# A new order for the first part of a Performer and Fourier-mixing kernel, from a planner with other costs and a lock list for the shared port

## The chip, the cores and the metric

The kernel runs on one core of one Trainium2 chip. The metric is the time of one execution on the device in microseconds (us). Before the change it is 1139.51 us, the median of three runs (1139.21 to 1140.97).

The engines of a core run side by side, each through its own list of instructions in order: TensorE (PE, matmuls; PEld is its weight load), VectorE (DVE), ScalarE (ACT) and GpSimd (POOL). SyncE (SP) is used as a queue that issues DMA transfers. An instruction that waits holds up all that stand behind it on its engine.

## What is computed

An attention block with positive random features, and a Fourier mixing block with a two-layer network behind it, all in float32, on 8 sequences of 576 tokens, 8 heads of 64 and a model width of 512:

```python
def phi(x):                                  # m = 128 features
    proj = np.einsum('bhsd,md->bhsm', x, omega)
    h = proj - np.sum(x * x, axis=-1, keepdims=True) / 2.0
    return np.exp(h - np.max(h, axis=-1, keepdims=True)) / np.sqrt(m)
q_p, k_p = phi(q * scale), phi(k * scale)
kv = np.einsum('bhsm,bhsd->bhmd', k_p, v)
z = np.sum(k_p, axis=2)
x = einsum('bhsm,bhmd->bhsd', q_p, kv) / (einsum('bhsm,bhm->bhs', q_p, z)[..., None] + 1e-06)
# heads side by side: x is (8, 576, 512)
u = x + np.real(np.fft.fft(np.fft.fft(x, axis=1), axis=2))
un = (u - mean(u)) / np.sqrt(var(u) + 1e-06)
out = u + np.maximum(un @ w_ch1, 0.0) @ w_ch2        # 512 -> 2048 -> 512
```

The weights w_ch1 and w_ch2 come as 64-bit floats and are narrowed to 32 bits on the chip.

## The kernel before

The work has two parts. The **first part** holds the attention of all 32 pairs of heads, the Fourier mixing of the 8 sequences, the narrowing of the weights, the network for the first 4 tiles of 128 tokens in the plain way, and the preparation of what the second part needs. The **second part** does the network for the other tokens in 8 blocks of 512, with a two-level scheme of sums and seven products in place of eight (lines L1454, L1596 and L1839 are its matmuls).

In the first part these streams run side by side:

- `attn` (three streams, pair n in stream n mod 3): q and k of a pair come in one tile `kq` and are transposed on TensorE (L524, groups of 4, 4 and 1 matrices), the transposed blocks are copied out of PSUM by ScalarE or VectorE (`evicted`, L538 and L540), projected on the features (`pairs_of`, L618), the row maxima are taken on VectorE (`softmax`, L561) and the exponentials on ScalarE (L578); the key-value products follow (L652) with a copy (`keep`, L666 and L668), the transposes of the query features (L524 again, out with `order`), the numerators and denominators (L699 and L707), and the division on VectorE or ScalarE (L716 to L728).
- `mix` (one stream over the 8 sequences): `folds` adds and subtracts rows on VectorE or GpSimd (L755 to L791), two rounds of matmuls with cosine and sine tables (L811 and L821, then L861 and L872), and `residual` adds the result to x (`summed`, L922 and L923) and stores u in DRAM.
- `weights` and `narrow`: 32 pieces of the weights are loaded as pairs of 32-bit words and put together by ScalarE or GpSimd, VectorE (L454 to L461), and a last add on GpSimd or VectorE (L467).
- `plain`: the network for the first 4 tiles, L1127 with w1 and L1150 with w2, with `hidden` between them (L1111 and L1113).
- `w2_parts`: differences of blocks of w2 for the second part (L1292, on VectorE or GpSimd), in seven sets; each set ends with five stores into `w2l` in DRAM from SyncE's queue (L1315 and L1317), and the next set rewrites the buffers that those stores read.
- `loads`, `loads_v`, `load_tables`: the loads of k, q, v (L388, L391, L396) and of the tables. `kq` has two buffers, v three.

TensorE uses different tile shapes for these steps, which the planner calls modes: "whole" (128x128: transposes, mixing, plain network), "rows" (64x128: projections of the first six pairs), "quarters" (64x64: the other projections and the key-value products) and "halves" (128x64: numerators, and the last part of a mixing).

The order of all instructions is set by hand-made planning. Each stream is a Python generator that yields a `Step` (engine or engines with a cost each, the events it waits for, buffers that it takes and gives, DMA size) and then writes its instructions. `Listing.run` keeps the list `todo` of the steps that stand next in each stream, chooses one, moves a clock for its engine, and lets the generator write the instructions, so that each engine's program is in the order of choice. In the first part the choice is not made by the clock but read from a string, `PICKS`: letter by letter, the index in `todo` is the letter's place modulo 36, and a letter of place 36 or more (a capital) sets `other`. Where a step may run on two engines, `other` chooses between them. In the second part there are no picks, and the step that can begin first is taken, within a slack, by its due time.

The clock still has a say in the first part where a step has two engines: before the change these are ranked by the time at which each would finish, and `other` takes the second of that rank. The clock's rows are in `FIRST`: the fourth figure, `turn`, is added to a TensorE step whose mode differs from that of the step before. Steps marked `port=True` read and write SBUF on VectorE or GpSimd; by `free[PORT]` none of them begins, in the planner's clock, before the one listed last has ended.

## Time and profile before

| what | value |
|---|---|
| median of three runs | 1139.51 us |
| the profiled execution's own time | 1138.29 us |
| its span | 1136.3 us |
| granted TensorE clock | 0.999 |
| first part on TensorE (start to the last L1150) | 0 to 421.5 us |
| busy in the first 423 us: PE, DVE, ACT, POOL | 410.6, 342.1, 281.1, 175.2 us |
| busy from 423 to 1136.3 us: PE, DVE, ACT, POOL | 705.5, 529.8, 263.4, 248.4 us |
| DMA, mean over the span | 227 GB/s |

The times of the profile count from the start of the span. A row of the chain of work that ended last gives a start, the time until the next piece of the chain, and the instructions in it. A row of waits gives the waiting engine, tile and line, what ended the wait, then the total, the number and the longest. A row of the order of time gives start and length. "Busy" for TensorE is modelled from the start of one matmul to the next and includes what a matmul is held up inside the engine.

### The profile page before, as it was taken

What the parts mean: (1) busy time and instruction counts of PE and PEld (TensorE: products, weight loads), DVE (VectorE), ACT (ScalarE), POOL (GpSimd) and SP (SyncE); (2) the same over time, 40 slices, a digit from 0 to 9 for tenths busy, and PEclk for the clock granted to TensorE, in tenths of its full rate; (3) what the DMA queues carried; (4) which work ended last, traced back from release to release, by engine and by line L of the source; (5) the groups of instructions that cost most, each with busy time, mean ns of one, the idle gap of its engine ahead of it and who ended that gap; (6) DMA issues with size and microseconds to landing.
All of it is one profiled execution on the core that took longest, in us unless ns stands there. A gap on an engine that the chain in (4) does not pass through costs nothing.

```text
span 1136.3 us, 34262 instructions
## 1 busy us (share of the span) xinstructions
PE 1116.1 (98%) x13639; PEld 1039.7 (91%) x13640; DVE 871.9 (77%) x1735; ACT 544.6 (48%) x1646; POOL 423.5 (37%) x435
## 2 busy tenths in 40 slices
PE   8999999999999999989999999999999999999998
PEld 7778888879868768989999999999999999999998
DVE  6999899987576646787777678678678678678666
ACT  7898898856535216724424424423523522522311
POOL 2443443553573124512711710720630540550361
PEclk9999999999999999999999999999999999999999
DMA  7856766575663238597797797798698798788576
GB/s 241 229 184 178 225 181 199 176 216 173 206 203 120 84 109 266 184 320 248 220 333 242 212 333 250 205 314 275 199 302 276 222 288 291 216 264 296 185 224 203
DMA packets 187965, 258.28 MB, mean 227 GB/s; under 512 B 52384, under 2 KB 83360, under 8 KB 187808
## 3 DMA queue, kind: packets, MB, share of 16 engines
q1 hardware_dynamic: 187312, 255.85, 72.2%
q8 instruction: 108, 1.77, 0.6%
q14 instruction: 49, 0.40, 0.1%
q10 hardware_dynamic: 496, 0.26, 0.1%
HBM read 212.27 MB, written 47.97 MB: 229 GB/s over the span
## 4 chain that ended last, share of the span: by engine, by line
PE 92%; DVE 2%; DMA 2%; ACT 2%; issue 1%; SPq 0%; POOL 0%; DVEq 0%; POOLq 0%
PE banks L1839 31%; PE banks L1454 27%; PE banks L618 5%; PE banks L1127 5%; PE banks L524 5%; PE banks L1150 4%; PE banks L1596 4%; PE banks L652 3%; PE banks L699 2%; PE banks L861 2%; PE banks L811 1%; DMA kq<-in_q_dram 1%; PE banks L821 1%; PE banks L872 1%; ACT e L578 1%
## 5 line engine op out<-in xcount | busy, mean ns | idle before, releaser
L1839 PE MATMUL banks<-wl,sums 128*128 128x128 f32 x1792 | 219.0, 275 | 3.3 <-issue 3.2
L1839 PEld LDWEIGHTS banks<-wl,sums 128*128 128x128 f32 x1792 | 209.3, 192 | 3.7 <-issue 3.7
L578 ACT ACTIVATE e<-banks,nmx 128x128 f32<-128x128 f32 x576 | 163.9, 421 | 23.0 <-DVE nmx L561 22.5
L1419 POOL TENSOR_TENSOR hid<-hid 128x512 f32<-128x512 f32 x98 | 128.8, 1318 | 118.7 <-ACT hid L1511 66.5
L1839 PE MATMUL banks<-wl,hid 128*128 128x128 f32 x1344 | 170.4, 275 | 0.4 <-DVE part L1817 0.4
L1839 PEld LDWEIGHTS banks<-wl,hid 128*128 128x128 f32 x1344 | 160.1, 192 | 0.6 <-DVE part L1817 0.6
L561 DVE TENSOR_REDUCE nmx<-banks 128x8 f32<-128x1024 f32 (+1 forms) x96 | 89.3, 951 | 18.8 <-PE banks L618 14.6
L1454 PE MATMUL banks<-rx,wx 128*128 128x128 f32 x672 | 88.8, 275 | 0.0
L1812 ACT ACTIVATE s<-banks 128x128 f32<-128x128 f32 x112 | 31.0, 277 | 109.4 <-PE banks L1839 89.1
L1497 DVE TENSOR_TENSOR hid<-banks,s 128x512 f32<-128x512 f32 x72 | 49.8, 691 | 42.9 <-PE banks L1454 35.6
L1454 PEld LDWEIGHTS banks<-rx,wx 128*128 128x128 f32 x672 | 81.8, 192 | 0.0
L618 PE MATMUL banks<-om,kqT 64*64 64x128 f32 (+1 forms) x2088 | 79.0, 275 | 1.3 <-ACT kv L668 0.7
L618 PEld LDWEIGHTS banks<-om,kqT 64*64 64x64 f32 (+1 forms) x2088 | 64.5, 138 | 12.3 <-issue 3.4
L1817 DVE TENSOR_TENSOR part<-banks,s 128x128 f32<-128x128 f32 x112 | 32.2, 289 | 48.6 <-PE banks L1839 47.0
L1127 PE MATMUL banks<-unT,w 128*128 128x128 f32 x512 | 65.4, 279 | 1.7 <-DVE qeT L538 1.7
L467 POOL TENSOR_TENSOR w<-w,raw 128x512 f32<-128x512 f32 x28 | 37.5, 1349 | 78.5 <-DVE raw L461 78.5
L1479 ACT ACTIVATE s<-banks 128x512 f32<-128x512 f32 x65 | 38.7, 595 | 57.4 <-PE banks L1454 56.9
L1127 PEld LDWEIGHTS banks<-unT,w 128*128 128x128 f32 x512 | 60.2, 192 | 4.4 <-issue 2.3
L1401 DVE CUSTOM_DVE_ANT_0 hid<-banks,s 128x512 f32<-128x512 f32 x63 | 43.6, 692 | 27.0 <-PE banks L1454 24.7
L1477 DVE TENSOR_TENSOR s<-banks,hid 128x512 f32<-128x512 f32 x70 | 48.4, 692 | 19.7 <-PE banks L1454 17.5
L1855 ACT ACTIVATE banks<-banks 128x128 f32<-128x128 f32 x56 | 14.7, 262 | 96.5 <-PE banks L1839 93.9
L1419 DVE TENSOR_TENSOR hid<-hid 128x512 f32<-128x512 f32 x90 | 57.5, 683 | 4.5 <-ACT hid L1550 4.5
(195 smaller groups left out, 2399.0 us busy)
## 6 DMA issues: line engine op xcount, KB each, us to landing
wl<-w2l SPq DMA_DIRECT2D x392, 256.0 KB
wx<-w1l SPq DMA_DIRECT2D x126, 256.0 KB
raw<-in_moe_w_ch_dram SPq DMA_DIRECT2D x32, 512.0 KB
kq<-in_k_dram SPq DMA_DIRECT2D x32, 288.0 KB
kq<-in_q_dram SPq DMA_DIRECT2D x32, 288.0 KB
vd<-in_v_dram SPq DMA_DIRECT2D x32, 288.0 KB
u<-us SPq DMA_DIRECT2D x36, 256.0 KB
ur<-us SPq DMA_DIRECT2D x36, 256.0 KB
```

Of the source, the lines that this page charges most:

```text
L524: nc.tensor.transpose(ps[:, (j - j0) * 128 : (j - j0 + 1) * 128], src(j), ident[:])
L561: nc.vector.tensor_reduce(nmx[:, :, 0:num], pps[:, :, 0 : MF * num].rearrange("p b (c m) -> p b c m", m=MF), axis=AX.X, op=ALU.max, negate ...
L578: nc.scalar.activation(out=e[:, c + (i if num == 1 else 0), :], in_=pps[:, i, MF * c : MF * c + MF], func=AF.Exp, bias=nmx[:, i, c : c + 1],)
L618: nc.tensor.matmul(pps[cols, c, MF * m : MF * m + MF], lhsT=kqT[rows, j, cols], rhs=om2[rows, :],)
L1127: nc.tensor.matmul(hp[:, 0:TP], lhsT=w1[:, dc, 128 * fc : 128 * fc + 128], rhs=unTs[key][:, dc, :], start=(dc == 0), stop=(dc == NDC - 1),)
L1150: nc.tensor.matmul(yp[:, 0:DM], lhsT=hs[fc][:, 128 * i : 128 * i + 128], rhs=w2[:, fc, :], start=(fc == 0), stop=(fc == NFC - 1),)
L1419: eng.tensor_tensor(out=o, in0=l, in1=r, op=op)
L1454: nc.tensor.matmul(ps[:, P * f : P * f + P].rearrange("f (b q) -> f b q", q=Q), lhsT=left[:, P * f : P * f + P], rhs=right, start=start an ...
L1477: nc.vector.tensor_tensor(out=s[:], in0=ps, in1=cell_of(addend, f, t), op=ALU.add)
L1497: nc.vector.tensor_tensor(out=o, in0=ps, in1=kept[saved][:], op=ALU.add)
L1596: nc.tensor.matmul(cell.rearrange("f t (b q) -> f t b q", q=Q), lhsT=w[:, d, col : col + 128], rhs=right[:, :, d].rearrange("f (t b) q -> ...
L1839: nc.tensor.matmul(ps[:, 0:128], lhsT=left[:, f], rhs=wls[j, i, n][:, f], start=start and f == 0, stop=(f == 3), skip_group_check=True,)
```

## The change

The string `PICKS` is another one of the same length, 1853 letters. With it the planner changes in these ways:

- `turn` in `FIRST` goes from 0.12 to 0.2, and TensorE's costs of six kinds of step change: a projection from 0.25 to 0.222 (rows) and 0.23 to 0.205 (quarters), the numerators from 1.22 to 1.165, a mixing step of the first round from 1.9 to 2.03, of the second from 1.38 to 1.46 and 0.94 to 0.91.
- The stores of a set of w2 sums are entered with 0.4 us of SyncE's queue, 1.0 us of latency and 300 KB in place of 3.0, 4.0 and 7 x 256.
- While picks are read, `other` now names an engine: the first or the second in the order in which the step lists them.
- While picks are read, a port operation takes the first gap that the other engine's port operations leave in the planner's clock (`unlocked`, over a list of the last 16 of that engine), and no longer waits for the port operation listed last.
- Where there are no picks, the rule is as before.

```diff
 FIRST = Clock(
-    270.0, 0.036, 0.2, 0.12, {PE: 0.163, ACT: 0.105, DVE: 0.085, POOL: 0.02}, {DVE: 0.12, ACT: 0.055},
+    270.0, 0.036, 0.2, 0.2, {PE: 0.163, ACT: 0.105, DVE: 0.085, POOL: 0.02}, {DVE: 0.12, ACT: 0.055},
     (PE, SP, NONE), {SP: 0.72, ACT: 2.9, PE: 1.1},
 )
 PICKS = (
-    "40e0f03eafdaegebg3NbcbeefdcOdeccfgdb37ghj0gjj7hlP79Kj7ik97i8S7efhjffeHldfPiehdjfdOShgihidaKOdbRhciff"
...
+    "002e03fbgebdfecNdebff9d3bgce8hdbbMabe3iMaPhaiheOhfb8f8bgibfO8eah9fbbf8ffa0bekg9ilTb9ffg9egihdhghed7c"
...
+LOCK = 1.0
...
+        self.locks = {DVE: [], POOL: []}
...
+    def unlocked(self, eng, t, length):
+
+        locks = self.locks[POOL if eng == DVE else DVE][-16:]
+        changed = True
+        while changed:
+            changed = False
+            for begin, end in reversed(locks):
+                if end < t - 8:
+                    break
+                if begin < t + max(length * LOCK, 1e-8) - 1e-9 and t < end - 1e-9:
+                    t, changed = end, True
+        return t
...
-    def start(self, step, ready, before, other=False, due=None):
+    def start(self, step, ready, before, other=None, due=None):
...
-            return max(t, u, self.free[e] if e != NONE else 0.0, self.free[PORT] if step.on_port(e) else 0.0)
-
-        engines = sorted(step.engines, key=lambda e: begin(e) + step.engines[e])
-        eng = engines[other and len(engines) > 1]
-        if due is not None and POOL in engines and due > self.front + AHEAD:
+            b = max(t, u, self.free[e] if e != NONE else 0.0)
+            if not step.on_port(e):
+                return b
+            return max(b, self.free[PORT]) if other is None else self.unlocked(e, b, step.engines[e])
+
+        if other is None:
+            eng = min(step.engines, key=lambda e: begin(e) + step.engines[e])
+        else:
+            eng = tuple(step.engines)[other]
+        if due is not None and POOL in step.engines and due > self.front + AHEAD:
...
-            other, n = divmod(DIGITS.index(pick), 36) if pick else (0, 0)
+            other, n = divmod(DIGITS.index(pick), 36) if pick else (None, 0)
...
             if step.on_port(eng):
                 self.free[PORT] = end
+                self.locks[eng].append((begin, end))
...
-                (0.25 if wide else 0.23) * len(js),
+                (0.222 if wide else 0.205) * len(js),
...
-            1.22,
+            1.165,
             mode="halves",
...
-                1.9,
+                2.03,
                 after=(("fold", b, n), name),
...
-                1.38 if c < NL else 0.94,
+                1.46 if c < NL else 0.91,
                 mode="whole" if c < NL else "halves",
...
-            yield Step(SP, 3.0, 4.0, after=(("w2t", i),), kb=7 * 256, makes=("w2l", i))
+            yield Step(SP, 0.4, 1.0, after=(("w2t", i),), kb=300, makes=("w2l", i))
```

## The prediction

> **What bounds the kernel now.** I read the page's busy shares first, then the chain of work that ended last, then TensorE's waits in the first part, then busy times by stretch, and last the order of time at the places where something stood still. A profiled execution of 1138.29 us (span 1136.3, 2.0 around it) is the base of the sum; the median of the three timed runs is 1139.51, so 1.2 us go on top at the end.
>
> ```profile
> PE 1116.1 (98%) x13639; PEld 1039.7 (91%) x13640; DVE 871.9 (77%) x1735; ACT 544.6 (48%) x1646; POOL 423.5 (37%) x435
> PE 92%; DVE 2%; DMA 2%; ACT 2%; issue 1%; SPq 0%; POOL 0%; DVEq 0%; POOLq 0%
> ```
>
> TensorE (PE) is the bound nearly everywhere: 92% of the chain. The change touches the list of the first part, which in the trace ends at 421.5 us with the last L1150 matmul. TensorE's waits in that part, all that are listed, and the busy times of five stretches of 40 us (columns: stretch, length, busy time and number of instructions of each engine, clock, DMA share, GB/s):
>
> ```profile
> PE banks L524 <- DMA kq<-in_k_dram: 2.3, 1, 2.3
> PE banks L524 <- DMA kq<-in_q_dram: 2.1, 2, 1.4
> PE banks L699 <- issue: 1.7, 1, 1.7
> PE banks L1127 <- DVE qeT L538: 1.7, 1, 1.7
> ```
>
> ```profile
> 40.00:80.00 40.00, 37.82 (x855) 32.15 (x854) 37.08 (x87) 37.02 (x138) 13.86 (x15) 1.00 0.66 189
> 80.00:120.00 40.00, 37.77 (x830) 31.93 (x833) 37.92 (x84) 33.54 (x118) 17.07 (x19) 1.00 0.68 211
> 120.00:160.00 40.00, 38.30 (x982) 33.81 (x971) 36.02 (x71) 34.49 (x128) 17.69 (x15) 1.00 0.56 170
> 160.00:200.00 40.00, 40.00 (x789) 35.68 (x790) 38.34 (x101) 35.39 (x128) 15.80 (x16) 1.00 0.72 214
> 200.00:240.00 40.00, 40.00 (x840) 32.74 (x837) 37.98 (x80) 29.50 (x103) 21.06 (x25) 1.00 0.63 196
> ```
>
> The reader is to see two things. TensorE stands still for only 12.4 us of 423 (423.0 less 410.6 busy), of which 3.3 are the start (waits at 1.0 and 9.2 us) and 1.0 the hand-over at 422; so a new order can win at most about 8 us of waits. And VectorE (DVE) is close behind: 37.08 + 37.92 + 36.02 + 38.34 + 37.98 = 187.3 of 200 us, 94%, while the clock is at 1.00 throughout.
>
> Busy is not all work, though. In the chain, the same groups have different lengths:
>
> ```profile
> 200.26 1.21 PE banks L652 x72
> 220.53 1.05 PE banks L652 x72
> 209.05 1.09 PE banks L1127 x8
> 280.96 1.79 PE banks L1127 x16
> ```
>
> The 72 key-value matmuls (64x64 tiles) take 1.05 us after other 64x64 matmuls and before more of them, 1.21 between groups of 128x128 tiles. Eight w1 matmuls (128x128) take 1.79 / 2 = 0.895 among their like, 1.09 between groups of other tile shapes. A visit to 64x64 between two 128x128 groups thus lengthens itself by 0.16 and the two half-edges of its neighbours by 0.195, 0.355 for two changes: **0.18 us a change of tile shape**. Going through TensorE's timeline up to 421.5 us and taking each step in the planner's mode, I count 170 stretches of one mode (75 whole, 58 quarters, 22 halves, 15 rows), 103 of them beginning in the five stretches above: 25, 20, 23, 19 and 16. 170 x 0.18 = 30.6 us of the first part is changing shape. This is the larger store.
>
> **The change part by part.** No instruction is added or removed: the steps are the same 1853 (both strings have 1853 letters), and what differs is the order in which each engine and each queue gets them and which of two allowed engines runs some of them. In the new string a capital means the second engine that a step names; there are 186. In the trace of before the second-named engine ran 183 steps (8 narrowings and 19 fold parts, 27 sums and 34 w2 sums on GpSimd; 4 last adds, 47 evictions and 20 hidden tiles on VectorE; 20 key-values and 4 normalisations on ScalarE). So the load of each engine stays about as it is, and the sum needs only order.
>
> *Fewer changes of shape.* The planner's price of a change goes from 0.12 to 0.2 us, against 0.18 in the trace, while its step costs fall by what they held of it (four projections of the late kind: 0.92 + 0.12 before, 0.82 + 0.2 after). So one change saved is now worth 1.7 times as much to whatever chose the order. How many go is not to be read from the string. Ends: +10 (nothing forces fewer), and -74: 32 head pairs need at least one quarter or row visit each and some 16 half visits, with as many whole ones between, 96 in all. In time +1.8 to -13.3 us. I take a third of the way to the far end, -25: projections and key-values of one pair are divided by a softmax, so that most visits in the trace stand apart for a reason. 25 x 0.18 = **-4.5 us**, all on the path, since TensorE is the path.
>
> *Ports.* The list before already let no port operation of VectorE begin before GpSimd's earlier listed one ended; now it may also go into a gap ahead of it. What such collisions cost is seen here, from the chain:
>
> ```profile
> 321.05 1.33 DVE x L922
> 322.38 1.40 DVE x L923
> 323.78 1.41 DVE u L1059
> 325.19 2.20 DVE half L755
> 327.40 1.15 DVE half L757
> ```
>
> Their groups' medians are 0.42, 0.42, 0.55, 1.22 and 0.16 us; each began while GpSimd held an add of 1.27 us, and the row lost about 5 us, of which 1.69 came out as TensorE's wait for L538 at 330.9, the last of the four waits above. Over the first part I find 23 VectorE instructions more than 0.15 us above their group's median, 13.9 us in all, mostly L454. Ends: -1.7 (this wait goes) and +2 (another such row falls before a softmax). The planner keeps the two apart only by its own clock; I take half of the gain, **-0.8 us**. [...]
>
> *The w2 stores.* The planner's price for the five stores after each set of w2 sums falls from 3.0 us of SyncE's queue, 4.0 of latency and 1792 KB to 0.4, 1.0 and 300 KB. The trace has:
>
> ```profile
> 277.40 2.29 SPq L1315 DMA_DIRECT2D w2l<-w  x3
> 279.79 1.60 SPq L1317 DMA_DIRECT2D w2l<-sums  x2
> ...
> 282.81 3.54 SPq L1315 DMA_DIRECT2D w2l<-w  x3
> 290.17 2.83 SPq L1317 DMA_DIRECT2D w2l<-sums  x2
> ```
>
> One group holds SyncE's queue for 4.0 us (277.4 to 281.4), another for 10.2 (282.8 to 293.0), with a v load next in the queue after the first and a q load after the other; the seven begin between 251 and 364. Behind them stand k, q and v loads, the stores and reloads of u, and the load of ur. With the new price each is listed 2.6 us (3.0 - 0.4) sooner after a group than before, and the data count for 300 / 270 = 1.1 us in place of 6.6. So TensorE may be listed to use a load that isn't there, and it waits in order. What covers it now: from issue to first use the late pairs 26, 27, 29, 30 and 31 have 12 to 37 us, pair 28 only 4.3. Ends: 0 and +8 (two loads late by 4 us each, the shortest group). One in the thin place late by 2.6, as likely as not: **+1.3 us**. The sums that rewrite the slabs also wait for these stores (GpSimd 4.7 us in one wait), but in this stretch it is half busy (21.9 of 40 us from 280, 20.9 from 320) and nothing of TensorE's first part reads them.
>
> *The rest.* Engine by name, the lock lists and the other TensorE prices are arithmetic of the planner; they act through the order alone. The second part's list is made by the same rule as before, from the times at which the first ends in the planner's clock; TensorE waits there 4.1 us (3.2 of them at 488), so I give it 0, with ends of -2 and +2.
>
> Sum: -4.5 - 0.8 + 1.3 = -4.0; 1138.29 - 4.0 = 1134.3 in the profile's terms, and 1139.51 - 4.0 = **1135.5 us**.
>
> **The rivals.**
> 1. *Loads late behind the w2 stores* (slower). Two loads on the path, late by 4 us each as the shortest group holds the queue, +8, less 4.5 of shape changes: 1139.5 + 3.5 = 1143; with three, 1147. It decides as soon as these waits pass 4.5 us. For it: prices far under the rows. Against it: only six pairs are still to load after 240 us, and five have 12 us or more in hand. Chance 0.20.
> 2. *Waits take back what the shape changes give.* Stretches of one mode are longer, so ScalarE and VectorE get their work in bursts; between 40 and 240 VectorE has 12.7 us left of 200, less than the -13.3 end would need. TensorE's 6.1 us of waits there grow by some 4: about 1139, within 0.2% (2.3 us, about what a measurement of this kernel can tell from no change). Chance 0.17. If they grow by 7 or more, by the same mechanism, 1142: chance 0.08.
> 3. *Both stores are emptied.* 50 changes fewer (-9.0) and most of the 8 us of waits gone through the ports (-3): 1127.5. [...] Against it: TensorE's longest other waits are for q loads (1.4 and 0.7 us), or for nothing that the profile shows (1.7). Chance 0.10.
> 4. *The order changes nothing that can be measured* because searches of so tight a list find other orders of equal worth; it ends where rival 2 ends and is in its 0.17.
>
> **How the numbers follow.** The forecast (fewer changes, waits about as now) has 0.45 and its own range of 1132 to 1137. Faster: 0.45 + 0.10 = 0.55; the same: 0.17; slower: 0.20 + 0.08 = 0.28. The range leaves out about a tenth at each end: below, half of rival 3, so to 1129.5; above, the worse part of rival 1, so to 1144.
>
> **What would show it.** In the new trace: fewer than 170 mode stretches in the first part (145 by my count), groups L652 x72 of 1.05 oftener than 1.21; the last L1150 ending near 417.5; TensorE's busy time about 4 us lower at the same number of matmuls, which can come from nothing but shape changes. Port step: fewer than 23 long VectorE instructions. Store step: a TensorE wait on a k, q or v load between 250 and 375 us. The prediction is wrong if busy time doesn't fall, or if the waits of the first part pass 17 us.

## The result and the profile after

The changed kernel takes 1155.46 us (median of five), the kernel before 1140.22 in the same session: a ratio of 1.0129 [1.0114, 1.0143], 14.7 us slower. The prediction, 1135.5, has the sign wrong. The profiled execution of after took 1152.9 us with a span of 1151.1; all lines of the code from L237 on stand 24 further down than before (L618 is now L642, L652 is L676, L1127 is L1151, L1150 is L1174).

The page's row of busy times, with its columns as before:

```profile
PE 1117.1 (97%) x13639; PEld 1042.0 (91%) x13640; DVE 869.9 (76%) x1724; ACT 549.6 (48%) x1665; POOL 445.1 (39%) x445
```

TensorE does the same work in the same busy time (1116.1 before) and stands still for longer. Its waits in the first part (total, number, longest):

```profile
PE banks L676 <- issue: 5.9, 4, 4.0
PE banks L548 <- DMA kq<-in_k_dram: 4.1, 1, 4.1
PE banks L676 <- DVE bmp L937: 1.9, 2, 1.1
PE banks L723 <- issue: 1.8, 2, 1.0
PE banks L548 <- DVE ur L1187: 1.1, 1, 1.1
PE banks L642 <- DVE kv L690: 1.1, 1, 1.1
PE banks L548 <- DVE kqT L562: 1.1, 1, 1.1
```

Two kinds have grown: waits on VectorE (3.1 us before, 5.7 now), and waits on "issue", for nothing that the profile shows (1.7 before, 7.7 now). Waits on DMA (4.4 and 4.1) and ScalarE (1.6 and 2.6) changed less. Summed over the matmuls' idle time, the first part's waits went from 11.8 to 21.1 us, and its hand-over to the second part from 422.5 to 431.6 us. The second part became 5.7 us longer as well (713.8 to 719.5). The five stretches of 40 us (stretch, length, busy time and instructions of each engine, clock, DMA share, GB/s):

```profile
40.00:80.00 40.00, 37.40 (x860) 32.65 (x862) 38.22 (x88) 33.62 (x117) 18.42 (x20) 1.00 0.61 173
80.00:120.00 40.00, 37.13 (x838) 31.84 (x833) 39.55 (x82) 34.75 (x127) 22.54 (x22) 1.00 0.75 220
120.00:160.00 40.00, 38.87 (x998) 34.86 (x990) 38.05 (x73) 33.75 (x120) 14.68 (x13) 1.00 0.65 194
160.00:200.00 40.00, 38.85 (x742) 33.96 (x740) 38.81 (x91) 33.01 (x124) 23.59 (x21) 1.00 0.53 162
200.00:240.00 40.00, 38.52 (x827) 32.02 (x825) 38.13 (x86) 31.36 (x110) 18.02 (x18) 1.00 0.70 220
```

From 160 to 240 us TensorE was busy 80.0 of 80 us before and is busy 77.4 now. VectorE went from 187.3 to 192.8 of the 200 us, with about as many instructions (419 and 416), and GpSimd from 85.5 to 97.2.

The longest stop comes at 268 us. TensorE in order of time there (start, length, work; in brackets the idle time before and what ended it), and SyncE's queue:

```profile
265.39 1.32 PE L642 MATMUL banks<-om,kqT 64*64 64x128 f32 x40
266.53 1.81 PE L676 MATMUL banks<-vd,e 64*64 64x65 f32 x110
272.29 1.34 PE L676 MATMUL banks<-vd,e 64*64 64x65 f32 x34 [3.95 <-issue]
```

```profile
256.47 2.80 SPq L1339 DMA_DIRECT2D w2l<-w  x3
259.37 1.67 SPq L1341 DMA_DIRECT2D w2l<-sums  x2
...
265.08 2.82 SPq L1339 DMA_DIRECT2D w2l<-w  x3
268.00 2.60 SPq L1341 DMA_DIRECT2D w2l<-sums  x2
```

TensorE stops in the middle of a group of key-value matmuls, with nothing to wait for. The page's DMA part gives away the cause (queue, packets, MB, share):

```profile
q8 instruction: 108, 1.77, 0.6%
```

These are packets of 16 KB (16,384 bytes each in the trace), 108 for TensorE's 27,824 records (27,279 matmuls and weight loads, 545 others), one for 258. Counted from the first record, the stop at 268 and five others each begin 193 behind a multiple of 256 (after 961, 1473, 2753, 5313, 10945 and 14017 records), and so does the one of the kernel before (5313). Each of the six ends 1.4 to 1.5 us after a packet has landed. Such stops take 9.0 us in after (1.2, 0.5, 1.0, 1.2, 4.2 and 0.8 us) and 1.9 us in the kernel before (one, at 130 us). Stops are counted here from the start of the last matmul before them, which is some 0.2 us more than the idle time in the rows: the one of 4.2 us is the row's 3.95. At 268 us the packet's transfer began only at 269.9 us, 1.8 us into the stop, on DMA engines full of w2 stores and loads. The windows of 4 us:

```profile
264.00:268.00 4.00, 4.00 (x156) 3.88 (x157) 2.19 (x6) 2.92 (x12) 2.80 (x3) 1.00 0.93 246
268.00:272.00 4.00, 0.34 (x22) 0.20 (x14) 0.27 (x2) 2.17 (x8) 2.19 (x2) 1.00 1.07 352
272.00:276.00 4.00, 3.71 (x48) 3.59 (x49) 1.07 (x5) 0.00 (x0) 1.06 (x1) 0.57 0.83 293
```

The DMA share is 1.07 in the stop, and behind it the granted clock is 0.57 for 4 us.

A measure that is used below is TensorE's progress: the time that the steps done so far would take at their shortest, without waits and changes of shape. After less before, it is -2.2 us at 20 us, -0.5 at 140, -2.2 at 180, -4.7 at 260, -9.5 at 280 and -10.2 at 400. The measure depends on what each step's shortest time is taken to be, and another choice of these times shifts it by 1 to 2 us; only its large steps are read here. Three places lose: the start (made good by 140 us), the stretch from 160 to 260, and the 20 us about the long stop.

### The profile page after: what moved, and what is told of

Its sections match the earlier page's. It is cut to its first block, busy times and chain, and to the rows that moved or that the text cites. A ratio compares the mean times of both kernels' runs of the same rounds, so it can differ in the third digit from the quotient of the medians.

```text
span 1151.1 us, 34257 instructions
## 1 busy us (share of the span) xinstructions
PE 1117.1 (97%) x13639; PEld 1042.0 (91%) x13640; DVE 869.9 (76%) x1724; ACT 549.6 (48%) x1665; POOL 445.1 (39%) x445
## 3 DMA queue, kind: packets, MB, share of 16 engines
q8 instruction: 108, 1.77, 0.6%
## 4 chain that ended last, share of the span: by engine, by line
PE 68%; DVE 1%; DMA 1%; issue 0%; ACT 0%; POOL 0%; DVEq 0%; POOLq 0%; ACTq 0%
PE banks L1863 30%; PE banks L1478 27%; PE banks L1620 3%; PE banks L1174 2%; PE banks L1151 2%; DMA u<-us 1%; PE banks L885 0%; PE banks L548 0%; PE banks L642 0%; PE banks L723 0%; PE banks L676 0%; PE banks L835 0%; DVE so L1443 0%; DVE hid L1443 0%; PE banks L896 0%
## 5 line engine op out<-in xcount | busy, mean ns | idle before, releaser
L642 PE MATMUL banks<-om,kqT 64*64 64x128 f32 (+1 forms) x2088 | 78.8, 276 | 1.6 <-DVE kv L690 1.1
L642 PEld LDWEIGHTS banks<-om,kqT 64*64 64x64 f32 (+1 forms) x2088 | 65.6, 140 | 11.4 <-issue 4.5
L1151 PE MATMUL banks<-unT,w 128*128 128x128 f32 x512 | 64.3, 279 | 0.1
L1425 DVE CUSTOM_DVE_ANT_0 hid<-banks,s 128x512 f32<-128x512 f32 x63 | 43.6, 692 | 26.6 <-PE banks L1478 24.3
L1151 PEld LDWEIGHTS banks<-unT,w 128*128 128x128 f32 x512 | 60.4, 193 | 2.4 <-issue 1.6
L1912 POOL TENSOR_TENSOR ur<-ur,part 128x512 f32<-128x512 f32 x21 | 27.3, 1304 | 88.8 <-ACT part L1905 83.3
L1069 POOL TENSOR_SCALAR rstd<-mv 128x1 f32<-128x1 f32 x28 | 6.2, 223 | 141.6 <-ACT junk L1065 139.8
```

Of the source, the lines that this page charges most:

```text
L642: nc.tensor.matmul(pps[cols, c, MF * m : MF * m + MF], lhsT=kqT[rows, j, cols], rhs=om2[rows, :],)
L1151: nc.tensor.matmul(hp[:, 0:TP], lhsT=w1[:, dc, 128 * fc : 128 * fc + 128], rhs=unTs[key][:, dc, :], start=(dc == 0), stop=(dc == NDC - 1),)
L1425: nc.vector._custom_dve(TENSOR_ADD_SAT, out=o, in0=ps, in1=sb, s0=FMAX, s1=0.0)
```

## The experiments

The theory after the two traces had four parts: the order's longer runs of small matmuls outrun the instruction supply (F), collisions of port operations hold VectorE up (P), the second part's list is worse (A), and the start is worse because the warm-up matmuls were moved. Rivals: VectorE simply has too much work (V), and the slack is taken back wherever something is mended. Ratios are to the kernel before in the same session; "first part" is the hand-over time in the profile.

| run | what it is | ratio [95%] | first part, us |
|---|---|---|---|
| after | the change | 1.0129 [1.0114, 1.0143] | 431.6 |
| e1 | after, second list of before | 1.0087 [1.0074, 1.0101] | 430.9 |
| e2 | after, warm-up first | 1.0131 [1.0116, 1.0145] | 430.2 |
| e3 | after, w2 stores apart | 1.0140 [1.0125, 1.0154] | 431.1 |
| e4 | before's order, new planner | 1.0053 [1.0038, 1.0068] | 420.8 |
| e5 | e1, 12 evictions to ScalarE | 1.0116 [1.0099, 1.0132] | 431.7 |
| e7 | before, 13 evictions to ScalarE | 1.0038 [1.0023, 1.0053] | 424.4 |
| e8 | e1 + warm-up + stores + evictions | 1.0155 [1.0136, 1.0173] | 438.8 |
| e9 | e1, burst split | 1.0079 [1.0058, 1.0100] | 430.9 |
| e10 | e9 + warm-up first | 1.0070 [1.0053, 1.0087] | 430.1 |
| e11 | e1, GpSimd's additions cut | 1.0037 [1.0022, 1.0051] | 427.2 |
| e12 | before, GpSimd's additions cut | 0.9981 [0.9969, 0.9993] | 418.1 |
| e13 | e10, loads ahead of w2 stores | 1.0135 [1.0112, 1.0157] | 434.5 |
| e14 | before, 10 changes of shape fewer | 1.0005 [0.9989, 1.0021] | 423.8 |

### The second part's list (e1) and the order alone (e4)

The second part has no string of picks; it is chosen by the planner's clock from the state in which the first part leaves it. By the planner's own arithmetic TensorE ends the first part at 510.7 us in before and 412.4 in after, and the other engines and buffers stand differently to it (the u of the last block 7.7 us behind TensorE before, 1.4 us ahead after). Run e1 sets that state as before's, which makes the second list equal to before's on every engine:

```diff
     listing.clock = SECOND
+    listing.made[("us", 7)] = listing.free[PE] + 7.7
+    listing.free[ACT] = listing.free[PE] - 13.7
+    listing.free[POOL] = listing.free[PE] - 16.8
...
+    listing.banks = [listing.free[PE] + d for d in (-14.2, -14.7, -13.5, 0.9, -13.6, -11.9, -12.1, -13.7)]
```

> The changed kernel with the planner's state at the hand-over (clocks of the engines, PSUM banks, the times of the last u stores and of the token sums) set as far from TensorE's clock as in the kernel before, so that the second part is listed instruction by instruction as before; the first part's list is the changed one. Theory A (the second part loses its 5.7 us because it is listed from another state): first part as in the changed kernel, 431 us, second part about 714 in place of 719.5, total 1155.5 - 5.7 = about 1150. Rival B (the second part loses because the first part leaves work on VectorE and the queues behind): second part stays near 719, total 1155.

Measured: 1.0087, so 0.0042, some 4.8 us with an uncertainty of 2.3, of the loss are the second list's. TensorE's waits from 430 to 600 us in after, and then in e1 (whose lines stand 9 further down from L1425 on):

```profile
PE banks L1620 <- ACT banks L1601: 3.5, 1, 3.5
PE banks L1863 <- ACT banks L1879: 2.7, 1, 2.7
PE banks L1863 <- ACT s L1836: 1.2, 1, 1.2
```

```profile
PE banks L1872 <- issue: 3.2, 1, 3.2
PE banks L1987 <- DVE ur L1187: 0.9, 1, 0.9
PE banks L1629 <- ACT banks L1610: 0.5, 1, 0.5
```

The wait of 3.5 us on ScalarE is 0.5 again, as before the change.

Run e4 tries the other half: before's 1853 choices of step and engine, written as a string for the new planner. Every engine's list of the first part is then before's, and only the second list is new.

```diff
 PICKS = (
-    "002e03fbgebdfecNdebff9d3bgce8hdbbMabe3iMaPhaiheOhfb8f8bgibfO8eah9fbbf8ffa0bekg9ilTb9ffg9egihdhghed7c"
...
+    "40e0f03eafdaegebg3NbcbeefdcOdeccfgdb37ghj0gjj7hlP79aj7ik97i8S7efhjffeHldffiehdjfdOihgihidaKedbhhciff"
...
```

> The changed kernel's planner with all its new costs, lock lists and engines by name, and in the string the order and the engines of the kernel before: the first part's lists are those of before on every engine, the second part is listed from the new planner's clock. Theory A (the order alone is what costs): first part 422.5, total 1140 plus what the second list is worth, up to 1145. Rival B (the planner's new costs cost by themselves, through the banks it hands out): first part over 425.

Its first part ends at 420.8 us, no later than before's, so the planner's new costs as such cost nothing there; and yet it is 1.0053. It isn't the mirror of e1, though. Its second list is neither before's nor after's but a third one: behind the hand-over VectorE has 980 instructions in before, 961 in after and 975 in e4, and e4's planner hands over with the u of the last block 7.7 us behind TensorE, as before's does. And what e4 computes is wrong, by a relative 0.13, though no instruction is left out; why is not known. So the price of after's second list rests on e1 alone. In e4's profile the second part takes some 2 to 3 us more than before's, once a stretch at half the clock is set aside.

### The start (e2) and the stores (e3)

```diff
 TensorE
+L519 Matmult banks<-ur_67 128x128 x6
 L548 Matmult banks<-ident,kq 128x128 x4
 L527 Matmult banks<-ident,om 128x128
 L548 Matmult banks<-ident,kq 128x128 x5
 L642 Matmult banks<-om_98,kqT 128x128 x18
-L519 Matmult banks<-ur_67 128x128 x6
```

> The changed kernel with one step moved on TensorE alone: the six warm-up products stand before the first transposes again, as in the kernel before, not after the first projections. Theory A (the first matmuls run slowly on a TensorE that has not been busy, and the warm-up itself lies on the path): the projections at 6.4 us take 2.0 in place of 3.6 and the 1.4 us of the warm-up lie in the wait for k, so 2.5 to 3 us less, about 1152.5. Rival B (the first k and q loads set the start whatever stands first): under 1 us, 1155.

TensorE's waits from 0 to 20 us in after, and in e2:

```profile
PE banks L548 <- DMA kq<-in_k_dram: 4.1, 1, 4.1
```

```profile
PE banks L548 <- ACT e L602: 1.4, 1, 1.4
PE banks L519 <- DVE ur L433: 1.0, 1, 1.0
PE banks L642 <- ACT e L602: 0.3, 1, 0.3
```

The start is mended: 14.2 us of work done at 20 us, where after has 11.5 and before 13.7, and 128.8 at 160 us (before 127.2, before's order in e4 129.3). So up to 160 us this order is no worse than before's. From 160 to 280 us it loses everything (230.0 against 237.5), and the total is unchanged at 1.0131.

```diff
 SyncE
+L420 DMACopy vd_101<-in_v_dram 128x9x64
+L420 DMACopy vd_99<-in_v_dram 128x9x64
+L420 DMACopy vd_100<-in_v_dram 128x9x64
+L412 DMACopy kq<-in_k_dram 128x576
 L1339 DMACopy w2l_121<-w_97 512x1x128 x3
 L1341 DMACopy w2l_121<-sums 128x2x512 x2
-L420 DMACopy vd_101<-in_v_dram 128x9x64
-L420 DMACopy vd_99<-in_v_dram 128x9x64
-L420 DMACopy vd_100<-in_v_dram 128x9x64
+L415 DMACopy kq<-in_q_dram 128x576
 L1339 DMACopy w2l_122<-w_97 512x1x128 x3
...
```

Later sets likewise; the w2 sums on VectorE and GpSimd move with their stores, TensorE's and ScalarE's lists stay.

> The changed kernel with the second and later sets of w2 sums and their stores listed later (the second store group some 18 us later in the planner's clock), TensorE's and ScalarE's lists untouched. TensorE's wait of 3.95 us at 268 ends 1.47 us after the landing of a 16 KB piece of TensorE's instructions, which began 1.8 us after TensorE had stopped, while the DMA engines were 107% busy with two store groups, k, q and u. Theory A (instructions come late because these transfers stand before them): that wait shrinks to under 1 us and the 4 us at a clock of 0.57 behind it go as well, 4 to 5 us less, about 1151. Rival B (144 small matmuls in a row use the instructions up faster than they can come, transfers or not): the wait stays above 3 us, total 1155.

The long stop shrank to 2.02 us, the clock behind it stayed at 1.00, and progress at 280 us is 232.3 us where after has 228.0, a gain of 4.3. All of it was given back: a wait of 1.7 us on ScalarE's exponentials came at 349 us, behind it the clock was at 0.50 from 349.5 to 352.9, which costs up to another 1.7, and the first part ended at 431.1. The stop is a true delay, and shrinking it alone is worth nothing.

### Is VectorE too full? (e5, e7, e8)

```diff
 VectorE
-L562 TensorCopy qeT<-banks 128x2x32 x2
 ScalarE
+L564 Activation qeT<-banks 128x2x32 x2
```

This at twelve places in e5, and at thirteen in the kernel before in e7.

> The changed kernel with the second part's list of before (as in the run that set it back alone, ratio 1.0087) and with 12 evictions of PSUM banks between about 73 and 240 us given to ScalarE in place of VectorE; TensorE's order is that of the changed kernel. Theory V, VectorE holds the first part back: it is busy 192.8 of the 200 us from 40 to 240 us in the changed kernel (187.3 before), and TensorE's pure work falls behind by 4.7 us between 0 and 260 us. About 0.45 us each makes 12 x 0.45 = 5.4 us less on VectorE; half of it, 2 to 3 us, should be seen in the end of the first part (near 428 in place of 430.9 us) and a ratio of about 1.006 to 1.007. Rival, it is the instruction fetch and the order itself that hold the first part: the end of the first part stays within 1 us of 430.9, ratio 1.008 to 1.010.

> The kernel before, all orders of TensorE, GpSimd and SyncE as they are, and 13 evictions of the first part (about 65 to 247 us) given to ScalarE in place of VectorE. Theory V: VectorE's 187.3 busy of the 200 us from 40 to 240 us already cost the kernel before something, so 1 to 2 us are gained, ratio 0.998 to 0.999, first part's end near 421 in place of 422.5 us. Rival, in the kernel before VectorE has enough left and ScalarE's evictions come later: no change, ratio 0.999 to 1.002.

Both were slower. VectorE's busy time from 40 to 240 us fell as meant (193.6 to 184.5 against e1, 187.3 to 180.6 against before), but the moved copies brought waits on ScalarE: in e7 1.7 us of them between 140 and 262 us, where before has no TensorE wait at all. The longest row from 60 to 262 us in e7:

```profile
PE banks L618 <- ACT kqT L540: 1.7, 2, 1.0
```

A copy put into ScalarE's list stands behind exponentials there. Theory V, that a sum of busy time is the limit, is not borne out: what counts is when a result comes, on two engines that are both nearly full (from 40 to 240 us VectorE was 92 and 90% busy in e5 and e7, ScalarE 84 and 87%).

> The changed kernel with four things set right at once: the second part's list of before (worth 4.8 us alone), the warm-up ahead of the first projections (3 us in the start, 0 to 1.4 in the total alone), the w2 stores of sets 2 and on later (4 us at 268 us, 0 in the total alone), and the 12 evictions moved to ScalarE. Theory, the four hide one another: each alone was given back in waits further on, together they add: 1155.5 - 4.8 - 1.4 - 4 - 2.5 = about 1143, ratio 1.001 to 1.005, end of the first part near 424 us. Rival, the slack is taken back at the same places whatever is mended: no better than the second list alone, ratio 1.007 to 1.010, end of the first part 429 to 431 us.

Four mends at once gave 1.0155, the worst of all, with the first part ending at 438.8 us and a wait of 2.7 us on ScalarE at 302 us, among others. Mends that each shift an engine's order don't add up.

### The instruction supply by itself (e6)

```diff
+    a = stage(1, a, w, False)
+    for t in range(36):
+        nc.sync.dma_start(scratch[128 * t : 128 * t + 128, :], a[:])
+    a = stage(2, a, w, False)
+    for t in range(36):
+        nc.sync.dma_start(outs[128 * t : 128 * t + 128], a[:])
+    a = stage(3, a, w, True)
```

> The whole computation is left out; three stages of TensorE work on zeros remain. 1: 60 groups of 36 small matmuls on 64x64 tiles, no transfers beside them. 2: the same beside 9.4 MB of stores. 3: 60 groups of 4 matmuls on whole 128x128 tiles beside 9.4 MB of stores. By the changed kernel's row of such small matmuls (2016 in 37.0 us, 18.4 ns each) stages 1 and 2 take 39.7 us each when nothing stops them, and 256 of TensorE's instructions, one packet of 16 KB, last 2.35 us. Theory F, TensorE runs out of instructions where small tiles follow one another beside transfers: stage 1 about 40 us with short stops at most; stage 2 longer, by 0.5 to 2 us for each of its 17 packets, 48 to 70 us; stage 3 without any such stop. Rival, the fetch keeps up whatever the transfers do and the stops have another cause: stage 2 within 1 us of stage 1.

Both were off in size, since the trace has two records for each float32 matmul (4320 for 2160), and theory F was off in its condition. The page's rows (busy time, mean ns, idle time before and its cause; stages 1, 2 and 3):

```profile
L32 PE MATMUL banks<-w 64*64 64x65 f32 x4320 | 72.5, 222 | 56.5 <-issue 50.8
L32 PE MATMUL banks<-w,next 64*64 64x65 f32 x4320 | 73.3, 224 | 55.1 <-issue 55.1
L38 PE MATMUL banks<-w,next 128*128 128x128 f32 x480 | 53.9, 275 | 0.7 <-ACT next L47 0.7
```

TensorE in order of time without transfers, and beside them:

```profile
80.58 2.09 PE L32 MATMUL banks<-w 64*64 64x65 f32 x128 [1.64 <-issue]
84.31 2.09 PE L32 MATMUL banks<-w 64*64 64x65 f32 x128 [1.64 <-issue]
...
133.33 2.09 PE L32 MATMUL banks<-w,next 64*64 64x65 f32 x128 [2.46 <-issue]
137.88 2.09 PE L32 MATMUL banks<-w,next 64*64 64x65 f32 x128 [2.46 <-issue]
```

128 matmuls and their 128 weight loads, one packet, run in 2.09 us, and then TensorE stops, in stages 1 and 2 for 105.9 us in 66 stops, in stage 1 with no transfer in the way but the packets themselves (DMA share 0.02). A packet comes each 3.45 to 4.0 us, mostly 3.45 or 3.73, and each 4.28 or 4.55 us beside the stores. So in e6 small tiles in a row use instructions at 8.2 ns each (2.09 us for 256) and are supplied at about 14 (3.45 or 3.73 us); transfers make it worse by up to a quarter but aren't the cause. The whole tiles of stage 3 have no such stop (0.7 us of idle time, before the first, for ScalarE). In the kernel, where other steps stand between, there are six such stops in after and one in before. Fewer changes of shape means longer rows: at 265 us two key-value groups and a projection follow one another in after.

### The burst split (e9), with the start (e10) and the loads (e13)

```diff
 TensorE
 L676 Matmult banks<-vd_100,e 64x65 x36
+L548 Matmult banks<-ident,e 128x128 x5
+L1151 Matmult banks<-unT,w_63 128x128 x4
 L676 Matmult banks<-vd_101,e 64x65 x36
-L548 Matmult banks<-ident,e 128x128 x5
-L1151 Matmult banks<-unT,w_63 128x128 x4
```

> The changed kernel with the second part's list of before (alone 1.0087), and TensorE's order changed at two places only, all other engines as they are: behind the first of the two key-value groups that follow one another near 265 us go 5 transposes and 4 products on whole tiles, and 4 such products go between two groups of small tiles near 362 us. Theory F, TensorE runs out of instructions: 256 of them last at least 3.5 us apart even without transfers (measured alone), so 9 matmuls more between the groups give the fetch 1 to 2 us, the stop of 4.46 us at 267 falls to 1.5 to 3 us, the first part ends near 428.5 in place of 430.9 us, ratio 1.006 to 1.008. Rival, the slack is taken back: the stop is shorter, and what was late before is waited for further on, as where the stores were moved apart: the first part ends within 1 us of 430.9, ratio 1.008 to 1.010.

> The run before it and the warm-up ahead of the first projections as well. Theory: the start is 2 to 3 us ahead (14.2 in place of 11.5 us of work done at 20 us), and as the largest stop is gone some of it stays: first part's end near 426.5, ratio 1.004 to 1.006. Rival: waits on VectorE and ScalarE from 160 to 260 us take the start's gain back (in the run with the warm-up alone they took 4.9 us against before's order): the first part ends as without it, ratio within 0.001 of the run before it.

The stop at 267 us went from 4.46 (e1) to 2.28 us (e9), as theory F said, and e10 stands at 232.4 us of progress at 280 where e1 has 228.2. But the first parts end at 430.9 and 430.1, and the ratios, 1.0079 and 1.0070, differ from e1's 1.0087 by no more than their intervals. What took it back first, from 273 to 300 us in e10:

```profile
PE banks L548 <- DMA kq<-in_k_dram: 1.2, 1, 1.2
```

A k load behind w2 stores, now that TensorE reaches it sooner. The next run put the v and k loads of that place ahead of the stores:

```diff
 SyncE
+L420 DMACopy vd_101<-in_v_dram 128x9x64
+L420 DMACopy vd_99<-in_v_dram 128x9x64
+L420 DMACopy vd_100<-in_v_dram 128x9x64
 L1339 DMACopy w2l_121<-w_97 512x1x128 x3
 L1341 DMACopy w2l_121<-sums 128x2x512 x2
-L420 DMACopy vd_101<-in_v_dram 128x9x64
-L420 DMACopy vd_99<-in_v_dram 128x9x64
-L420 DMACopy vd_100<-in_v_dram 128x9x64
```

> The run with the split burst, the warm-up first and before's second list (1.0070), and the w2 stores of its second set and later ones behind the v and k loads of their place (about 5 us later at first, less further on); TensorE's and ScalarE's orders stay. That run lost at 272 and 288 us what it had ahead: 3.11 us for instructions and 1.25 us for a k load, both behind w2 stores on the DMA engines (95 to 107% busy from 256 to 284 us). Theory, the transfers of that stretch are the bound: both waits shrink to under 1.5 us together and 2 us of it stay, first part's end near 428, ratio 1.004 to 1.006. Rival: the slack is taken back by ScalarE and VectorE further on as where the stores alone were moved (1.7 us at 349 us): end 429.5 to 430.5, ratio 1.006 to 1.0085.

The instruction stop shrank to 1.29 us and the load's wait went, yet the run is slower than both its theories, 1.0135. TensorE's waits from 260 us on in e13:

```profile
PE banks L548 <- ACT e L602: 4.7, 2, 4.5
PE banks L548 <- DVE big L1316: 1.7, 1, 1.7
PE banks L676 <- issue: 1.1, 1, 1.1
```

The w2 sums came later along with their stores, and what stands behind them came later too:

```profile
281.63 1.27 POOL L1316 TENSOR_TENSOR sums<-w 128x512 f32<-128x512 f32 x1 [13.02 <-DMA w2l<-sums]
...
290.75 2.27 DVE L779 TENSOR_TENSOR half<-x 128x1024 f32<-128x1024 f32 x1 [5.96 <-POOL mid L815]
```

A sum on GpSimd waits 13 us for the stores that free its buffer. The mixing's copy L815 stands behind it on GpSimd, VectorE waits 6 us for that copy, and the softmax's maxima stand behind this on VectorE; ScalarE's exponentials and then TensorE's 4.5 us follow from there. From 295.8 us the clock was at half for 6.8 us. From 256 to 300 us transfers, w2 sums and attention are packed so that each mend makes the next one late.

### The port (e11, e12)

Both runs let GpSimd's additions compute one column of each row, and leave out the others, so that GpSimd is busy for less time (from 140 to 260 us 29.5 us in place of 55.2 on the changed order, 34.6 in place of 57.5 on before's).

```diff
+        if step.eng == POOL:
+            dst, lof = dst[:, 0:1], lof[:, 0:1]
         eng.tensor_tensor(out=dst, in0=dst, in1=lof, op=ALU.add)
...
+            k1, k2 = (1, KD + 1) if step.eng == POOL else (KD, DM)
-            eng.tensor_tensor(out=u[:, 0:KD], in0=u[:, 0:KD], in1=left[:, 0:KD], op=ALU.add)
+            eng.tensor_tensor(out=u[:, 0:k1], in0=u[:, 0:k1], in1=left[:, 0:k1], op=ALU.add)
```

> Leaves work out: of GpSimd's additions of the weights' halves and of the Fourier sums only one column of each row is computed, on top of the changed kernel with the second part's list of before (1.0087); all orders are as they are. Theory P, the port: 9 of the first part's 22 us of VectorE's long instructions lie beside these additions (4.4 of 13.9 us in the kernel before), and VectorE is busy 19.2 of each 20 us from 140 to 240 us, so 2 to 4 us of TensorE's waits there go: first part's end 426 to 429 us, ratio 1.004 to 1.007, and the gain is at least 2 us larger than that of the same cut in the kernel before. Rival: the waits of that stretch come from the order of the steps and not from the port: VectorE's busy time falls and TensorE waits on, gain under 1 us or the same in both kernels.

> Leaves out the same as the run before it, in the kernel before: the control. Theory P: 0 to 1.5 us gained, as there 4.4 us of long VectorE instructions lie beside these additions and TensorE waits for no engine from 140 to 260 us: ratio 0.9985 to 1.000. Rival, GpSimd's additions being short is worth the same in both: 2 to 4 us, ratio 0.9965 to 0.998.

Measured: 0.0050 gained on the changed order (1.0087 to 1.0037, 5.7 us), 0.0019 on before's (2.1 us). The difference, 3.6 us with an uncertainty of about 2.7, is what these additions cost the new order more than the old. It isn't shown that collisions make this difference: the cut also shortens GpSimd's own work, and in the profiles the first part, where all the cut work lies, became shorter by 3.7 us in the new order (430.9 to 427.2) and by 4.4 in the old (422.5 to 418.1). Run e12's 0.9981 lies between the ranges of its two expectations. From 140 to 260 us, in e1, e11, before and e12 (columns as above):

```profile
140.00:260.00 120.00, 116.67 (x2369) 96.33 (x2371) 114.08 (x243) 94.67 (x339) 55.15 (x52) 1.00 0.55 170
```

```profile
140.00:260.00 120.00, 118.52 (x2399) 99.16 (x2398) 110.41 (x247) 97.49 (x353) 29.47 (x52) 1.00 0.59 179
```

```profile
140.00:260.00 120.00, 120.00 (x2427) 99.85 (x2420) 112.12 (x241) 97.06 (x343) 57.51 (x56) 1.00 0.66 200
```

```profile
140.00:260.00 120.00, 120.00 (x2478) 100.16 (x2477) 108.03 (x241) 97.69 (x345) 34.64 (x59) 1.00 0.64 192
```

VectorE's busy time falls by 3.7 and 4.1 us. In the new order 1.9 us of it turn up as TensorE's work, in the old one none, since TensorE wasn't waiting there. In after a collision looks like this (GpSimd's last add of one narrowing beside VectorE's middle of the next):

```profile
184.42 0.43 DVE L478 TENSOR_SCALAR sign<-raw 128x512 uint32<-128x512 uint32 x1
184.47 1.52 POOL L491 TENSOR_TENSOR w<-w,raw 128x512 f32<-128x512 f32 x1 [4.78 <-DVE raw L485]
184.88 1.66 DVE L480 SCALAR_TENSOR_TENSOR w<-w,sign 128x512 uint32<-128x512 uint32 x1
```

The same L480 takes 0.69 us at 189.56, beside no add; the row at 184.88 is about 1 us longer, beside an add of 1.52.

### Fewer changes of shape alone (e14)

```diff
 TensorE
+L618 Matmult banks<-om_98,kqT 128x128 x10
+L524 Matmult banks<-ident,e 128x128 x8
-L618 Matmult banks<-om_98,kqT 128x128 x2
-L524 Matmult banks<-ident,e 128x128 x4
-L618 Matmult banks<-om_98,kqT 128x128 x8
-L524 Matmult banks<-ident,e 128x128 x4
```

One of six such places is shown; every other engine's list is before's.

> The first step of the change alone: in the kernel before, 6 of TensorE's steps are moved past 1 to 3 others, so that 10 changes of tile shape fewer remain (of 170); every other engine's list and the second part are word for word those of before. At 0.18 to 0.19 us each this is 1.9 us. Theory, a change of shape costs what was measured and nothing takes it back where bursts, ports and transfers stay as they are: ratio 0.998 to 0.999, first part's end 420.5 to 421.5 us against 422.5. Rival, each step that comes earlier meets an input that isn't there, as the kernel before has no slack: ratio 1.000 to 1.003, new waits on VectorE or ScalarE of 2 us or more behind the six places.

170 stretches became 160, and the ratio is 1.0005 [0.9989, 1.0021]: at best 1.3 us faster, not 1.9. Among TensorE's waits in the first part stand three that before hasn't:

```profile
PE banks L1127 <- ACT e L578: 0.6, 1, 0.6
PE banks L699 <- ACT qeT L540: 0.6, 1, 0.6
PE banks L811 <- ACT qeT L540: 0.5, 1, 0.5
```

They sum to 1.7 us, about what ten changes should give, but they aren't the explanation: the one instruction stop is 0.9 us shorter and other waits shrank, so that the first part's waits sum to 11.8 us as before. This execution also ran at half the clock from 9.7 to 13.1 us, which costs up to 1.7. Without waits and that loss the first part takes 410.4 us where before takes 410.8, so that the ten changes bought about 0.4 us of the 1.8 that the prediction's price gives them; and the eleven timed runs show no gain.

## Why the prediction was wrong

**Fewer changes of shape, -4.5 us.** The count was right: 141 stretches, where 145 were foreseen. The price of 0.18 us was not. From 40 to 160 us it seems to hold: net of waits, TensorE's time over its steps' shortest times went from 16.1 to 13.65 us there with 68 and 55 stretches, 0.19 us each. But two executions of before's order, before and e4, differ by 1.4 us in that same stretch; from 160 to 200 us the excess rose from 3.5 to 4.6 us with four stretches fewer, and in e14 it fell by only 0.2 us from 40 us on, with five fewer. Over the whole first part, without waits and without what half the clock took, before's order takes 410.8 to 412.3 us (before, e4, e7) and the new one 408.9 to 410.6 (after, e1, e2, e3, e5): 29 changes fewer bought some 1 to 2 us, where the price makes it 5.2. So one step that failed is the size of this term. The other is "all on the path, since TensorE is the path": busy time didn't fall (1116.1 to 1117.1), and the first part's waits grew by 9.3 us, to 21.1, past the 17 that the prediction named as its refutation. The list of four waits that it called all sums to 7.8 of 11.8 us. With the waits counted, the first part of after is 9.1 us longer than before's. Run e14 shows that even ten changes saved with nothing else touched gain nothing that can be measured. That a step put beside its like then comes earlier than its input, or another one later, fits the new waits, but no run isolates it.

**Ports, -0.8 us with ends of -1.7 and +2.** Wrong in direction: long VectorE instructions of the first part rose from 23 to 37 and from 13.9 to 21.9 us. That only 1.69 of the 13.9 us came out as a wait of TensorE was true of an order in which TensorE waits for nothing from 140 to 260 us, and I carried it over to one in which it waits. What that costs TensorE is open: e11 and e12 give 3.6 us more than before, with an uncertainty of 2.7, and the first parts of their profiles show none of it. That the planner's list keeps the two apart "only by its own clock" was said, and half of the gain was taken all the same; its clock ends the first part at 412 us, the chip at 431.6. On the chip a VectorE instruction beside one of GpSimd's adds still lasts longer (1.66 us for L480 at 184.88, 0.69 beside none): the list doesn't keep the two apart there.

**The w2 stores, +1.3 us.** Place and mechanism were right, the victim was not. Between 250 and 375 us no matmul of after waits for a k, q or v load. The packet of instructions came late behind the same stores, a stop of 4.17 us. The loads stood next in the row, as e9 and e10 showed with 1.2 us on a k load. Rival 1, at 1143, had the sign and too small a size, for the wrong reason.

**The second part, 0 with ends of -2 and +2.** This term was mis-sized: 4.8 us by e1, with an uncertainty of 2.3, and 5.7 in the two profiles (713.8 to 719.5). I took "made by the same rule" for "the same", although the times that the rule starts from were among the things that changed.

**What was left out.** Instruction supply was no term at all, though the one long "issue" wait of before, 1.7 us, was among the four lines shown and called a wait for nothing that the profile shows. The clock was no term either: in after one window at half the clock, behind the long stop, takes back 1.6 us, and the mean clock of after's five timed runs, 0.996 where before's have 0.998, is some 2.3 us of the loss. The warm-up's move was not seen either; it cost 2 to 3 us in the start, which would have been taken back by 280 us in any case (e2).

**The sum.** Of 14.7 us, about 5 are the second list's. The other 9 or 10 lie in the first part, most of them between 160 and 300 us, where short waits on VectorE and ScalarE, the instruction stop, late loads and half the clock take each other's place; what the port has of them is not settled. Runs e2, e3, e9, e10 and e13 each shorten one and see it again in another; how the time divides among them stays open. Rival 2 (waits take back what the shape changes give, at 1142 in its worse form) named that mechanism. No version of the new order beat the kernel before, and of before's own variants e14 is the same and e7 slower; e12 is faster only because it leaves work out.

## What to carry to other kernels

A cheaper neighbour is worth its price only where the moved step has slack, and in a list whose engines are all near full, ten such savings made alone gave nothing that could be measured: check the planner's clock against the trace (412 to 431.6 us here) before trusting what it promises. Count instructions as well as time: in e6 small matmuls use 256 in 2.1 us and are supplied with 256 per 3.45 to 4.0 us, and longer rows of small tiles have that price beside the changes of shape that they save (stops of 9.0 us in after, 1.9 before). And where a later stage is planned from the state in which an earlier one ends, pin that state or cost the later stage anew; here it was about a third of the loss.

## What was unexpected in the hardware

- TensorE's instructions arrive by DMA in packets of 16 KB (108 in after, 16,384 bytes each); the six stops of after lie multiples of 256 records apart, and in e6 256 instructions, run in 2.09 us, stand between two stops. In e6 the transfer of a packet begins about 1 us after TensorE has gone on with the one before, takes 0.9 to 1.4 us, and TensorE goes on 1.2 to 1.6 us after it has landed, so that one comes each 3.45 to 4.0 us with the DMA engines nearly idle (DMA share 0.02), and each 4.28 or 4.55 beside stores (0.91 to 1.05). In after a packet's transfer began 1.8 us into the stop.
- In these traces half the clock comes in windows of 3.41 us, and how a stop lies in them made a difference. In after the granted clock changes at 272.09, 275.50 and 1149.31 us, 1 and 256 times 3.41 us apart. There the window from 268.67 to 272.09 has TensorE busy for 0.00 us, and the next one a granted clock of 0.50 (the 0.57 above is this, averaged over 4 us). The window before was not always wholly idle: 0.83 us busy in e2 (268.87 to 272.28, a stop of 3.37 us) and 0.95 in e6 (139.43 to 142.84) were followed by 0.50 as well. But e5's stop of 3.66 us lay across two windows, with 1.62 and 1.77 us busy, and the clock stayed at 1.00. In after and before half the clock followed windows that were busy for 0.00, 0.34 and 0.36 of their length (after from 268.67, before from 1131.42, after from 1145.90 us) and not those with 0.43 and 0.45 (before from 486.31, after from 439.34); in e8 and e3 it followed one with 0.44 and one with 0.50.
- With the same second list, the second part's length in the profiles lies between 713.8 and 718.2 us (before, e1, e5, e7 to e14), so that a difference of less than some 4 us there can't be read from one profile; the second list's cost rests on the timed runs. Part of that spread is the clock: the runs with a window at half the clock there (e5, e8, e9, e11, e12, e13) have 716.1 to 718.2 us, the others 713.8 to 716.1.
